# Attention and SwiGLU block: four pairs loaded in natural order and turned by TensorE, fewer transfers, reciprocals between transposes

## The chip, the core and the metric

The program runs on one core of one Trainium2 chip. A core has TensorE (PE), VectorE (DVE), ScalarE (ACT), GpSimd (POOL) and SyncE (SP), which only issues transfers here. Each engine works through its own instructions in the order in which they were written; semaphores order the engines among each other. The metric is device time in microseconds (us) of the core, the median of several runs.

## The reference

Normalised attention for 8 batches, 12 heads, 448 tokens and 64 features per head, and then a gated feed-forward layer over the 3584 tokens with 768 features (hidden width 1536). Cut to what is computed:

```
def rmsnorm(x, g):
    rms = np.sqrt(np.mean(x * x, axis=-1, keepdims=True) + 1e-06)
    return x / rms * g
q_n, k_n = (rmsnorm(q, g_q), rmsnorm(k, g_k))
scores = np.matmul(q_n, k_n.transpose(0, 1, 3, 2)) / np.sqrt(64)
scores = scores - np.max(scores, axis=-1, keepdims=True)
attn = np.exp(scores)
attn = attn / (np.sum(attn, axis=-1, keepdims=True) + 1e-09)
x = np.matmul(attn, v)            # then (B,H,S,D) -> (B*S, H*D)
g = x @ w_gate
out = (g / (1.0 + np.exp(-g)) * (x @ w_val)) @ w_out
```

Inputs and output are float32, but the three weight matrices arrive as float64.

## The kernel before

All work is in the function `fast`; `general` is another path, taken only if the gains are large, and does not run here.

**Pairs.** Two heads of one batch make a pair; `attention(m)` makes the work of pair m, of 48. The first 12 (`EARLY`) are done before any product of the feed-forward layer; the other 36 are spread among the down products of earlier blocks. Two batches form a block (`NB` is 4).

**One early pair.** `load` (L728) brings queries and keys in four transfers each, 56 KB apiece, in runs of 32 features (128 bytes), so that 32 tokens lie on 32 partitions and the head's feature halves in partition groups. `load_values` (L744, L747) brings values in four transfers. ACT squares both (L754), DVE sums over 32 features (L768), ACT swaps the sums of the feature halves between partition groups (L778), DVE adds them (L782). `inverse_root` takes a logarithm and an exponential on ACT (L678, L679) and improves the result on DVE (L684 to L686). POOL scales keys and queries (L795), DVE turns them in 32x32 blocks (L811), and ACT multiplies the queries by the gains (L814). Then come the scores on TensorE (L840) in four steps, the exponentials on ACT (L855), the weighted sums of the values (L916) and the sums of the weights (L947). DVE takes reciprocals of those (L982), TensorE spreads them over partitions (L990; in later pairs ACT does it, L1000), and the result is copied (L1005), joined (L1008) and divided (L1012) into `xs`.

**Buffers.** Queries and keys have four tiles (two pairs), values two, turned queries and keys two each. The score tile `st` has two buffers of two PSUM banks each; `at` for weighted sums has two of one bank; two more banks, `banks`, serve the sums of early pairs and later the gate products.

**Weights.** `convert` brings nine blocks of 128x128 float64 weights (1152 KB) in five transfers (L1136, L1138) into one of several places (`XS`, `GT`, `HS`, `ES`, `PAIRS`, `SPARE`), turns them into rounded float32 on ACT and DVE (L1146 to L1180), builds eleven sums and differences of blocks on POOL (L1199, L1202), and stores 15 "sides" to DRAM (L1227). There are 24 such pieces, sixteen for the up and eight for the down products; six of them are planned among the early pairs. A place can be used again when its sides are stored; some places wait for the last sums of the early pairs, since attention uses that memory.

**Blocks.** A 3x3 block product is done in 15 products. `block(n)` loads sides (L1288) in groups of five for the up products (L1328) and of two for the down products (L1502), and reads and combines the products on ACT and DVE.

**What sets the order.** The class `Order` keeps a list of pieces, each with an engine, an estimated time, a wished time (`when`) and a rank. A simulated run over these estimates picks, at each step, the piece that can start first, and ties go to the smaller `when - rank`. The instructions are written in the order in which it picks them, so an estimate changes the order, not only the prediction of it. `LEAD` is the planned start of the first pair, `PAIR` the planned time of an early one. Weight pieces of the early stage have rank 0, early pairs 60.

Of the kernel before, what the change touches and what calls it, by code (L numbers as in the profile page):

```python
# [477 lines left out]
def fast(  # L478
# [59 lines left out]
    EARLY = 2 * NPAIR  # L538

# [7 lines left out]
        qk=4, v=2, t=2, QT=2, KT=2, e=4, ea=7, eh=2, sums=1, inv=1, rd=1, rows=3, st=2, at=2, ss=2,  # L547
# [18 lines left out]
    def take(name, key, shape):  # L566
        if name in ("e", "ea"):
            at = order.turn[name] % BUFS[name]
            tiles[name, key] = es[:, at] if at < BUFS["e"] else more_es[:, at - BUFS["e"]]
            return tiles[name, key]  # L570
# [38 lines left out]
    UP_SUMS = (8, 1, 7, 13, 10, 14, 3, 5, 11, 0, 4)  # L609
    DOWN_SUMS = (1, 10, 14, 3, 11, 0, 4, 5, 8, 7, 13)  # L610
    BLOCKS = (6, 2, 12, 9)
# [16 lines left out]
    chosen = const.tile([P, 2, P], F32, name="chosen")  # L628
    gq2 = const.tile([P, 1], F32, name="gq2")
# [6 lines left out]
    LEAD, PAIR = 14.0, 9.0  # L636
# [35 lines left out]
    def inverse_root(m, sums, of, when, rank=0.0):  # L672


        def estimate():
            ss = of()
            rr = take("rr", m, list(ss.shape))
            nc.scalar.activation(rr, ss, AF.Ln, scale=GAIN**-2)  # L678
            nc.scalar.activation(rr, rr, AF.Exp, scale=-0.5)  # L679
# [18 lines left out]
    clusters = {}  # L698

# [3 lines left out]
    def attention(m):  # L703
# [19 lines left out]
        def load(x, src):  # L723
            def emit():
                to = take("qk", (m, x), [P, NC, C])
                for g in range(P // C):
                    rows = src[b, 2 * c + g // 2][:, ts(g % 2, C)]
                    queue.dma_start(to[ts(g, C)], rows.rearrange("(c i) f -> i c f", i=C))  # L728
# [5 lines left out]
                "ACT" if both else "SP", 1.4 if both else 2.4, ready - 28.0, emit, takes=[("qk", (m, x))], kb=224, early=25.0,  # L734
                after=[staged.get(PAIRS)],
            )

        loaded = [load(x, src) for x, src in enumerate((q, k))]
# [10 lines left out]
        load_v = add("SP", 2.4, ready - 16.0, load_values, takes=[("v", m)], kb=256, early=25.0)  # L749

        def square(x):
            if x == 0:
                take("t", m, [P, 2, NC, C])
            nc.scalar.activation(tiles["t", m][:, x], tiles["qk", (m, x)], AF.Square)  # L754
# [12 lines left out]
        def summed():  # L767
            nc.vector.tensor_reduce(  # L768
# [20 lines left out]
        sums = add("ACT", 0.9, ready - 16.0, swap, after=[sums], uses=[("ss", m)])  # L789
        sums = add("DVE", 0.15, ready - 15.0, both, after=[sums], uses=[("ss", m)])  # L790
        rr = inverse_root(m, sums, lambda: tiles["ss", m][:, 0], ready - 14.0, rank)

        def scale(x):
            rr = tiles["rr", m][:, ts(x, NC)].rearrange("p (c one) -> p c one", one=1)
# [13 lines left out]

        def transpose(x):
# [9 lines left out]
        kt = add(  # L819
# [3 lines left out]
        qt = add(  # L823
# [3 lines left out]
        qt = add(  # L827
# [81 lines left out]
        def weighted(j):  # L909
            for x in range(2):  # L910
# [4 lines left out]
                for h in range(2):  # L915
                    nc.tensor.matmul(  # L916
                        tiles["at", (m, x)][ds(D * h, D), queries],
                        tiles["v", m][rows, j, h],
# [39 lines left out]
        for j in range(NJ):  # L958
# [5 lines left out]
                uses=[weights_of(j), ("v", m)] + at * (j > 0),  # L964
# [16 lines left out]
        def invert():  # L981
            nc.vector.reciprocal(take("rd", m, [P, Q]), tiles[den])  # L982
# [27 lines left out]
        def divide():  # L1010
# [8 lines left out]
            "DVE", 1.52, when + 4.0, invert, after=[all_sums], uses=[] if of_bank else [den],  # L1019
            takes=[("rd", m)],  # L1020
# [99 lines left out]
    def convert(key, src, sums, to, when, place, by_bank):  # L1120

        rank = 20.0 if by_bank else 0.0
# [4 lines left out]
        raw, dst = places[place][:, 0 : 2 * VALUES], places[place][:, 2 * VALUES : PLACE]  # L1127
        words = raw.bitcast(U32).rearrange("p (n two) -> p n two", two=2)
        lo, hi = words[:, :, 0], words[:, :, 1]
        wait = [last_exp[0]] if place in (ES, PAIRS, GT[2]) else []  # L1130

        def load():

            to = raw.bitcast(I64).rearrange("p (b f) -> p b f", f=P)
            for i, n, rows in ((0, 2, (1, 3, 0)), (2, 2, (0, 2, 2)), (5, 3, (0, 3, 1))):
                nc.sync.dma_start(to[:, i : i + n], src(slice(*rows[:2]), rows[2]))  # L1136
            for i, k, n in ((4, 0, 0), (8, 2, 2)):
                nc.sync.dma_start(to[:, i], src(k, n))  # L1138

        loaded = add(  # L1140
            "SP", 2.5, when - 12.0, load, after=[staged.get(place), *wait], kb=1152, early=3.0
# [50 lines left out]
        b21, b31, b13, b23, b11, b12, b22, b32, b33 = (blocks[:, i] for i in range(9))  # L1192

        sides = places[place].rearrange("p (b f) -> p b f", f=P)[:, 7:22]
        at = {x: i for i, x in enumerate(sums)}
# [8 lines left out]
        def pair(x, i, j):  # L1204
            return x[:, i : j + 1 : j - i]
# [4 lines left out]
        for us, op in (  # L1210
            (0.79, plus(pair(sides, at[10], at[4]), pair(blocks, 5, 7), pair(blocks, 2, 8))),
            (0.79, plus(pair(sides, at[1], at[14]), twice(w[10]), pair(blocks, 0, 4))),
# [8 lines left out]
            (0.79, minus(pair(sides, at[11], at[0]), pair(blocks, 7, 8), pair(blocks, 2, 3))),  # L1221
# [56 lines left out]
    def load_sides(key, sides, part, sums):  # L1278
# [4 lines left out]
        for names, first in ((sums, 0), (BLOCKS, len(sums))):  # L1283
            here = sorted(names.index(x) for x in part if x in names)
            if here:
                size = len(here)
                src = sides[:, ds(first + here[0], size)]
                nc.sync.dma_start(to[:, ds(i, size)], src.rearrange("p x a b f -> p x (a b f)"))  # L1288
                i += size

    def place_of(x, part, sums):
        mine = [*(y for y in sums if y in part), *(y for y in BLOCKS if y in part)]
        return mine.index(x)
# [303 lines left out]
    for t, x in ((gq2, g_q), (gk2, g_k)):  # L1597
        col = x.rearrange("(d one) -> d one", one=1)
        nc.gpsimd.dma_start(t[0:64, :], col)
        nc.gpsimd.dma_start(t[64:128, :], col)  # L1600
    nc.vector.memset(chosen, 0.0)
# [96 lines left out]
```

## Time and profile before

| what | us |
|---|---|
| median of 3 runs | 1487.12 |
| lowest and highest | 1483.69, 1489.3 |
| span of the profiled execution, first to last instruction | 1484.0 |
| TensorE busy in it | 1425.0 (96%) |
| DVE, ACT, POOL busy | 916.0, 681.5, 414.1 |

The profile is of one further execution; its own device time is not listed apart from its span, which lies within the three runs. Busy time of TensorE counts from a matmul's start to its modelled end. A wait names the instruction that came last before the waiter could go on.

The order of the stages can be read off the timeline: no TensorE work until 14.66 us, the twelve early pairs until about 140 us, the up products of block 0 until about 330 us with most of the weight conversion beside them, then four stages in which down products and later pairs alternate with up products, and the last down products until about 1476 us.

### The profile page before, as it was taken

To read this page: it belongs to the slowest core of one execution; us is meant where nothing else is said; L and a number is where in the kernel's file an instruction comes from. 1 tells how busy PE (TensorE), PEld (TensorE's weight loads), DVE (VectorE), ACT (ScalarE), POOL (GpSimd) and SP (SyncE) were. 2 spreads that over 40 slices of the span, in tenths; PEclk is the share of its full clock that TensorE was granted. 3 is DMA by queue.
4 is the path that set the end of the run, shared out by engine and by line. 5 is a ranking of instruction groups with operands and counts; after the bars stand their busy time and mean duration, and the time that the engine had idled before them with its cause. 6 is when DMAs were issued, how large, how long until landed. Compare 5 with 4: busy or idle time off the path is not lost.

```text
span 1484.0 us, 19470 instructions
## 1 busy us (share of the span) xinstructions
PE 1425.0 (96%) x6672; PEld 675.4 (46%) x6672; DVE 916.0 (62%) x1405; ACT 681.5 (46%) x1366; POOL 414.1 (28%) x468
## 2 busy tenths in 40 slices
PE   5789999999999999999999999999999999999998
PEld 2334544443444455544444445554444445555553
DVE  4777887877978544355886733454786854432533
ACT  6774544437775322445767422354676532122100
POOL 2454586636444100012544200011343410000000
PEclk9999999999999999999999999999999999999999
DMA  7767999974453432533344432352353442222235
GB/s 165 158 144 236 292 308 341 296 219 90 99 115 85 113 106 71 138 103 90 74 111 110 100 117 73 106 136 77 96 119 85 90 119 89 80 98 73 83 98 107
DMA packets 415921, 193.30 MB, mean 130 GB/s; under 512 B 324164, under 2 KB 397892, under 8 KB 409668
## 3 DMA queue, kind: packets, MB, share of 16 engines
q1 hardware_dynamic: 402688, 190.35, 48.0%
q10 hardware_dynamic: 12996, 1.61, 0.7%
q8 instruction: 55, 0.90, 0.3%
q14 instruction: 54, 0.44, 0.1%
q0 software_dynamic: 128, 0.00, 0.0%
HBM read 157.29 MB, written 34.60 MB: 129 GB/s over the span
## 4 chain that ended last, share of the span: by engine, by line
PE 73%; DVE 3%; ACT 2%; issue 1%; DMA 1%; SPq 1%; ACTq 0%; DVEq 0%
PE mm L1502 22%; PE mm L1328 20%; PE at L1328 20%; PE st L840 6%; PE at L916 5%; PE st L947 1%; ACT spare L1000 1%; ACT es L855 1%; DVE rd L982 1%; DMA out_dram<-spare 0%; SPq L728 0%; DVE ss L782 0%; DMA work<-in_k_dram 0%; DVE ss L768 0%; DVE sums L866 0%
## 5 line engine op out<-in xcount | busy, mean ns | idle before, releaser
L1328 PE MATMUL mm<-xs,ws 128*128 128x448 f32 x960 | 401.2, 540 | 4.4 <-DVE spare L1276 2.2
L1328 PE MATMUL at<-xs,ws 128*128 128x448 f32 x960 | 400.6, 540 | 4.1 <-DVE v L1274 2.6
L1328 PEld LDWEIGHTS mm<-xs,ws 128*128 128x128 f32 x960 | 181.5, 190 | 185.8 <-issue 173.8
L1328 PEld LDWEIGHTS at<-xs,ws 128*128 128x128 f32 x960 | 181.9, 190 | 184.6 <-issue 172.6
L795 POOL TENSOR_TENSOR work<-work,rr 128x448 f32<-128x448 f32 x96 | 105.9, 1122 | 503.5 <-DVE rr L686 245.2
L840 PE MATMUL st<-work 64*64 64x448 f32 (+1 forms) x1536 | 155.1, 508 | 27.3 <-ACT work L814 21.2
L1502 PE MATMUL mm<-gt,ws 128*128 128x448 f32 x448 | 177.2, 545 | 0.0
L1272 DVE TENSOR_TENSOR gt<-gt,mm 128x448 f32<-128x448 f32 x64 | 39.7, 621 | 185.1 <-PE mm L1328 171.3
L1502 PE MATMUL mm<-hs,ws 128*128 128x448 f32 x384 | 152.1, 545 | 0.9 <-DVE ss L684 0.9
L855 ACT ACTIVATE es<-st 128x896 f32<-128x896 f32 x129 | 114.3, 913 | 56.1 <-PE at L916 42.8
L860 POOL TENSOR_TENSOR sums<-es 128x896 f32<-128x896 f32 x36 | 75.7, 2104 | 195.8 <-PE st L947 83.2
L1402 ACT ACTIVATE st<-gt 128x448 f32<-128x448 f32 x96 | 52.4, 547 | 163.8 <-DVE gt L1276 85.9
L1000 ACT COPY spare<-rd 32x224 f32<-32x224 f32 x288 | 108.1, 375 | 35.0 <-DVE rd L982 30.7
L1502 PEld LDWEIGHTS mm<-gt,ws 128*128 128x128 f32 x448 | 82.9, 190 | 84.2 <-issue 81.0
L916 PE MATMUL at<-es,v 64*64 64x448 f32 x1032 | 110.2, 545 | 7.2 <-ACT xs L1005 3.3
L1270 ACT COPY gt<-mm 128x448 f32<-128x448 f32 x80 | 42.5, 531 | 141.5 <-PE mm L1328 141.4
L1502 PEld LDWEIGHTS mm<-hs,ws 128*128 128x128 f32 x384 | 71.1, 190 | 72.9 <-issue 70.9
L840 PEld LDWEIGHTS st<-work 64*64 64x64 f32 x1536 | 50.9, 134 | 108.7 <-issue 38.1
L1270 ACT COPY v<-at 128x448 f32<-128x448 f32 x96 | 51.1, 532 | 83.2 <-PE at L1328 80.0
L860 POOL TENSOR_TENSOR sums<-sums,es 128x896 f32<-128x896 f32 x36 | 78.7, 2187 | 2.8
L811 DVE STREAM_TRANSPOSE work<-work 128x448 f32<-128x448 f32 x96 | 59.2, 627 | 25.2 <-POOL work L795 23.1
L916 PEld LDWEIGHTS at<-es,v 64*64 64x64 f32 x1032 | 39.7, 134 | 67.4 <-issue 57.4
(150 smaller groups left out, 1568.7 us busy)
## 6 DMA issues: line engine op xcount, KB each, us to landing
ws<-up_sides SPq DMA_DIRECT2D x32, 1024.0 KB, 4.9
ws<-down_sides SPq DMA_DIRECT2D x16, 1024.0 KB, 5.0
ws<-down_sides SPq DMA_DIRECT2D x28, 512.0 KB, 4.0
ws<-up_sides SPq DMA_DIRECT2D x16, 768.0 KB, 4.6
work<-in_q_dram SPq DMA_DIRECT2D x192, 56.0 KB, 2.4
work<-in_k_dram SPq DMA_DIRECT2D x188, 56.0 KB, 2.5
out_dram<-spare SPq DMA_DIRECT2D x168, 56.0 KB, 1.9
v<-in_v_dram SPq DMA_DIRECT2D x96, 96.0 KB, 2.5
```

The lines of the kernel that those rows point to most:

```text
L795: nc.gpsimd.tensor_tensor(out=tiles["t", m][:, x], in0=tiles["qk", (m, x)], in1=rr.to_broadcast([P, NC, C]), op=ALU.mult,)
L811: nc.vector.transpose(to, tiles["t", m][:, x].rearrange("p c f -> p (c f)"))
L840: nc.tensor.matmul(st[ds(D * x, D), h, 0:n], tiles["KT", m][rows, ds(P * j + D * of_keys, D)], tiles["QT", m][rows, ds(Q * of_queries, n)] ...
L855: nc.scalar.activation(e, tiles["st", (m, j)][:, :, 0 : S * width(j) // P], AF.Exp)
L860: nc.gpsimd.tensor_tensor(out=to, in0=tiles["e", (m, 0)] if j == 1 else to, in1=e, op=ALU.add)
L916: nc.tensor.matmul(tiles["at", (m, x)][ds(D * h, D), queries], tiles["v", m][rows, j, h], tiles["e", (m, j)][rows, h], start=j == 0, stop= ...
L1000: nc.scalar.copy(inv[ds(D * h + C * to, C), ts(x, Q)], tiles["rd", m][ds(D * h + C * x, C)])
L1270: nc.scalar.copy(to, ps)
L1272: nc.vector.tensor_tensor(out=to, in0=old, in1=ps, op=ALU.add)
L1328: nc.tensor.matmul(ps(), w[:, at, which, c], xs[:, SLOT[x], c], start=fresh and c == 0, stop=c == NC2 - 1, skip_group_check=True,)
L1402: nc.scalar.activation(take(*act, [P, 2, TB])[:, 0, 0:S], to, AF.Silu)
L1502: nc.tensor.matmul(banks[s][:, 0:S], w[:, at, s, g], where[x][:, g], start=fresh and g == 0, stop=g == NG - 1, skip_group_check=True,)
```

## The change

Six things are changed at once.

1. **Natural order for pairs 0 to 3.** Four tokens lie on one partition (112 partitions, each with 4 x 64 features of each head), so queries and keys are one transfer each, in runs of 1 KB. A token's features are on one partition, so nothing is swapped. POOL scales and sorts by token index, TensorE turns four 112x128 pieces of each into a PSUM tile `st`, and DVE (keys) and ACT (queries, with the gains) drain them.
2. **A few products ahead.** In pair 0, four products of the raw keys into a bank that nobody reads are issued on TensorE after the second square.
3. **Values for three pairs at a time** in the early stage: five transfers for three pairs, into `spare`.
4. **Weights in three transfers** per piece instead of five; raw and rounded parts change places, and the sides get another order, which gives fewer transfers in one of three groups of up sides. The sixth early piece goes to `GT[0]` instead of `SPARE`, which now waits for the last sums. Early weight pieces get rank 30.
5. **Reciprocals** (all 48 pairs): DVE turns the sums, takes reciprocals of seven columns, and turns them back, spread out.
6. `LEAD` is 10 instead of 14, and some estimates differ.

The core of the diff:

```diff
+    NATURAL = (0, 1, 2, 3)
+    R = S // NJ
...
-    UP_SUMS = (8, 1, 7, 13, 10, 14, 3, 5, 11, 0, 4)
-    DOWN_SUMS = (1, 10, 14, 3, 11, 0, 4, 5, 8, 7, 13)
-    BLOCKS = (6, 2, 12, 9)
+    UP_SUMS = (10, 14, 3, 8, 1, 7, 13, 5, 11, 0, 4)
+    DOWN_SUMS = (3, 10, 14, 1, 11, 0, 4, 5, 8, 7, 13)
+    BLOCKS = (6, 9, 2, 12)
...
-    LEAD, PAIR = 14.0, 9.0
+    LEAD, PAIR = 10.0, 9.0
...
+                if natural:
+                    to = take("qk", (m, x), [R, 2, NJ * D])
+                    rows = src[b][2 * c : 2 * c + 2].rearrange("h (p j) d -> p h (j d)", j=NJ)
+                    queue.dma_start(to, rows)
+                    return
...
+        def load_six():
+            x = take("ve", m // 3, None)
+            for j in range(NJ):
+                for p in (0, D) if j == NJ - 1 else (0,):
+                    n = D if j == NJ - 1 else P
+                    rows = v[b][2 * c : 2 * c + 6, ds(P * j, n)].rearrange("h s d -> s h d")
+                    nc.sync.dma_start(x[ds(p, n), j], rows)
...
+            nc.scalar.activation(tiles["t", m][:, x], of, AF.Square)
+            if m == 0 and x:
+                for _ in range(4):
+                    nc.tensor.matmul(banks[0], chosen[0:R, 0], of, start=True, stop=True)
...
+        def turn(x):
+            if x:
+                take("st", (m, "turned"), [P, 2, TB])
+            turned = tiles["st", (m, "turned")][:, x]
+            for j in range(NJ):
+                nc.tensor.transpose(turned[:, ts(j, R)], tiles["t", m][:, x, ts(j, P)], ident[0:R, 0:R])
+
+        def drain(x):
+            turned = tiles["st", (m, "turned")][:, x, 0:S].rearrange("p (j r) -> p r j", j=NJ)
+            to = take("KT" if x else "QT", m, [P, S]).rearrange("p (r j) -> p r j", j=NJ)
+            if x:
+                nc.vector.tensor_copy(out=to, in_=turned)
+            else:
+                nc.scalar.activation(to, turned, AF.Copy, scale=gg)
...
         def invert():
-            nc.vector.reciprocal(take("rd", m, [P, Q]), tiles[den])
+            rd, rc = take("rd", m, [P, Q]), take("rc", m, [P, Q // C])
+            nc.vector.transpose(rd, tiles[den])
+            nc.vector.reciprocal(rc, rd.rearrange("p (c i) -> p c i", i=C)[:, :, 0])
+            every = rc.rearrange("p (c one) -> p c one", one=1).to_broadcast([P, Q // C, C])
+            nc.vector.transpose(rd, every)
...
-        rank = 20.0 if by_bank else 0.0
+        rank = 20.0 if by_bank else 30.0
...
-            for i, n, rows in ((0, 2, (1, 3, 0)), (2, 2, (0, 2, 2)), (5, 3, (0, 3, 1))):
-                nc.sync.dma_start(to[:, i : i + n], src(slice(*rows[:2]), rows[2]))
-            for i, k, n in ((4, 0, 0), (8, 2, 2)):
-                nc.sync.dma_start(to[:, i], src(k, n))
+            for at, n in ((slice(3, 8, 2), 0), (slice(0, 3), 1), (slice(8, 3, -2), 2)):
+                nc.sync.dma_start(to[:, at], src(slice(0, 3), n))
...
-    turns = [(*XS, *GT[:2], HS, SPARE), (ES, PAIRS, GT[2], SPARE, HS), (ES, PAIRS, HS, SPARE), (ES, HS)]
+    turns = [(*XS, *GT[:2], HS, GT[0]), (ES, PAIRS, GT[2], SPARE, HS), (ES, PAIRS, HS, SPARE), (ES, HS)]
```

## The prediction

> **What bounds the kernel now.** I read busy time by stretches first, because the change sits almost wholly in the first twelve pairs. Columns: stretch, length, then busy time and count for PE, weight loads, DVE, ACT and POOL, granted clock, DMA share, GB/s.
>
> ```profile
> 0.00:15.00 15.00, 0.34 (x4) 0.30 (x8) 5.62 (x18) 6.55 (x18) 4.72 (x14) 1.00 0.67 114
> 15.00:140.00 125.00, 105.21 (x1196) 46.51 (x1189) 94.56 (x156) 86.24 (x163) 61.80 (x93) 0.99 0.72 174
> 140.00:333.00 193.00, 185.75 (x492) 92.37 (x490) 156.90 (x236) 86.00 (x122) 112.42 (x218) 1.00 0.95 292
> 333.00:400.00 67.00, 63.70 (x434) 26.37 (x438) 57.06 (x79) 50.99 (x119) 39.28 (x24) 1.00 0.46 97
> 400.00:1400.00 1000.00, 993.44 (x4353) 471.49 (x4346) 569.42 (x880) 447.49 (x937) 195.86 (x120) 1.00 0.38 98
> ```
>
> From 400 to 1400 us TensorE rests 6.6 us in all, so nothing there can give much. It rests 14.7 us before its first product, 19.8 us in the twelve early pairs (15 to 140), 7.3 us in the first up products, and 7.4 us in the tail of stores. Those first two are where the change can act. Next, the lead, from the timeline (start, length, engine, line):
>
> ```profile
> 5.85 0.58 ACT L754 ACTIVATE work<-work 128x448 f32<-128x448 f32 x1 [2.96 <-DMA work<-in_k_dram]
> 7.15 0.58 ACT L754 ACTIVATE work<-work 128x448 f32<-128x448 f32 x1 [0.73 <-DMA work<-in_k_dram]
> ...
> 8.88 0.88 ACT L778 COPY ss<-ss 32x28 f32<-32x28 f32 x4 [1.15 <-DVE ss L768]
> ...
> 11.39 1.83 POOL L795 TENSOR_TENSOR work<-work,rr 128x448 f32<-128x448 f32 x2 [7.79 <-DMA v<-in_v_dram]
> ...
> 12.50 1.40 DVE L811 STREAM_TRANSPOSE work<-work 128x448 f32<-128x448 f32 x2
> ...
> 13.94 0.67 ACT L814 ACTIVATE work<-work,gg 128x448 f32<-128x448 f32 x1 [0.44 <-DVE work L811]
> ```
>
> One serial chain, begun by a load. Then what TensorE waited for from 14 to 140 us (total, times, longest; the 14.7 is the lead):
>
> ```profile
> PE st L840 <- ACT work L814: 21.2, 6, 14.7
> PE at L916 <- ACT xs L1005: 3.3, 2, 2.3
> PE at L916 <- DVE xs L1008: 2.7, 2, 2.1
> PE at L916 <- ACT gt L855: 2.3, 2, 1.3
> PE mm L990 <- DVE rd L982: 2.0, 2, 1.3
> ```
>
> ACT is named, but is it the cause? The timeline around the stall at 44.39 (2.10 us) shows ACT standing still for a load, and SP issuing that load late:
>
> ```profile
> 36.90 4.15 SPq L728 DMA_DIRECT2D work<-in_k_dram  x4
> ...
> 41.50 0.58 ACT L754 ACTIVATE work<-work 128x448 f32<-128x448 f32 x1 [1.01 <-DMA work<-in_q_dram]
> 43.20 0.58 ACT L754 ACTIVATE work<-work 128x448 f32<-128x448 f32 x1 [1.13 <-DMA work<-in_k_dram]
> 43.69 0.65 ACT L814 ACTIVATE work<-work,gg 128x448 f32<-128x448 f32 x1
> ```
>
> Pair 3's queries stood on ACT behind pair 4's squares. Summed over its timeline, SP spends 111.0 of the first 128 us issuing (55.5 of the first 60): 54.8 on 92 queries-and-keys transfers, 31.6 on 48 of values, 17.9 on 30 of weights. SP's queue is what the early pairs wait for underneath; DVE (94.6 of 125) is next.
>
> [...] pair 0's first 448-column records take 951 ns, later ones 536; about 4 us of half speed lose 2.0. [...]
>
> **The change, part by part.**
>
> *Lead.* A pair's tensor becomes one transfer of 1 KB runs, not four of 128 B. Queries: issued by 0.76 + 0.57 (4.58 / 8), plus the 2.8 us from last issue to square today (3.05 to 5.85): 4.1. Keys on ACT: 1.63 + 0.57 + 2.8 = 5.0. Second square 0.58 x 512/448 = 0.66, to 5.7. Reduction 1.09 x 1024/896 = 1.25, to 7.0. The swap (0.88) goes; a small add of 0.19 takes the place of L782. Root and its three corrections, 10.02 to 11.17 today, to 8.5. POOL 0.92 x 512/448 = 1.05 each: keys 9.7, queries 10.7. The warm-up (4 products of 512 columns; L1328 gives 0.376 a record of 448, two records each) costs 3.4 us warm and 6.9 cold, 5.5 when 4 us are cold: 5.0 to 10.5. It stands ahead of the first transposes in PE's order: keys turned 10.5 to 11.5, queries to 12.4, ACT's drain 0.66, scores at about **13.0** instead of 14.66: 1.7 won, plus the 2.0 of half clock, since the array is then warm. Identity building on POOL (after its fourth gain transfer, 3.6) has until 9.7; were that cover gone, each us is a us.
>
> *TensorE's transposes.* Four a turn. Nearest row: L990, 128x128 weights by 224 columns, four records in 0.95 us (28.22 to the next), 0.24 each. One record per transpose gives 0.95 a turn, two give 1.9. I take 0.95 [...], so 1.9 a pair; pairs 1 to 3 add **5.7**, at worst 11.4. Pair 0's lie in the lead.
>
> *SP.* Queries and keys lose 21 issues x 0.60 = 12.5; values go from 48 issues to 4 x 5, 28 x 0.66 = 18.4; six weight pieces lose two each, 12 x 0.60 = 7.2. Some 38 of 111 us leave the queue. What is late next is DVE.
>
> *DVE and ACT.* Each reciprocal (1.55) becomes two 224-wide transposes (0.627 / 2 + some 0.02, so 0.33) and a 7-column reciprocal (0.19, like the small L684): 0.87, 0.68 less; twelve times, 8.2. Natural pairs swap two DVE turns (1.25) for one copy (0.64): 2.4. ACT loses four swaps, 3.5. DVE falls from 94.6 to some 84. Bounds of the triple: 0.6 to 1.6, so from 11 won to nothing.
>
> *TensorE's rests, 15 to 140.* L814: 6.5 without the lead (21.2 - 14.7). Of these 5.5 are stalls at 21.28, 33.29, 44.39 and 58.33 (0.85 + 0.29 + 2.10 + 2.58, less some 0.3 kept), all behind late loads: gone. L855 loses half (1.2), L982 loses 0.6 twice (1.2). L1005 and L1008 (6.0, ACT and DVE late between pairs 4 and 7) lose half, 3.0. Together 10.9, leaving 8.9. If only the load stalls go, 14.3 stay; if nearly all go, 3.
>
> *End of the early stage.* 13.0 + 105.2 - 2.0 + 5.7 + 8.9 = **130.8** against 140.0: 9.2 won.
>
> *Later.* Weight conversions after the early pairs wait for the last sums (SP waited 9.0 us for L947), so block 0's preparation shifts with it. Three transfers carry the same bytes as five: nothing, hidden by a DMA share of 0.95; SP's spared issuing there has no taker. The regrouped sides save one transfer in each up triple: nothing, since TensorE waited 0.9 us for these. The placing of the sixth weight piece in GT[0] makes it wait for the first piece's store; if it is late, 1 to 3 us. Steady state: L982 delayed L840 by 1.3 us in all: 1.3 won. Total 10.5.
>
> Span 1484.0 - 10.5 = 1473.5. The median shown is 1487.1, 3.1 above the span, so **1476.6**.
>
> **The rivals.**
> - *Absorbed in block 0.* The pairs end early, but the weights (0.95 of the DMA engines from 140 to 333) set the pace, and TensorE waits for sides instead. For: share and 292 GB/s. Against: only 0.9 us of such waits now, and a rigid shift. Some 3 us left: 1484.
> - *Fuller.* Rests fall to about 2 and no transposes' cost is visible: 7 more than mine, and up to 3 of DVE relief: 1467. For: SP and DVE both relieved. Against: ACT still in order between squares and exponentials.
> - *Slower: the turned pair holds a score tile.* Both turns write one of the two two-bank tiles `st`, from the first transpose to ACT's drain, over 3 us with the queries' scaling between. Scores and exponentials then alternate on one tile: 0.76 + 0.92 + 0.3 instead of 0.95 a step, 1.05 x 4 steps = 4.2 a pair, and with two records per transpose 1.9 more: 6.1 x 4 = 24 against 10.5 won: about 1500. It decides from 10.5 / 4 = 2.6 us a pair. For: PE is in order, and only two tiles. Against: weighted sums and totals can run meanwhile, and TensorE has 20 us of rest.
>
> **How the numbers follow.** Mine 0.50 (its own range 1470 to 1482: transposes twice as dear +5.7, rests -6 to +5), absorbed 0.18, fuller 0.16, slower 0.16. 0.5% is 7.4 us, about what a measurement can tell from no change; faster means below 1479.7. Mine is that nine times in ten (0.45), fuller always, so 0.61, with a little of the absorbed 0.62; same 0.22; slower 0.16. Range 1464 to 1488: it leaves out the slower case and little of the fuller.
>
> **What would show it.** First scores near 13 us and records of 536 ns there; transposes near 0.24 us each; SP issuing some 73 us in the early stage; three DVE instructions of 0.87 for each reciprocal; first up product near 131 us; unchanged rests from 140 to 333, shifted. Wrong if scores wait for `st`, if the first up product is past 138, or if TensorE waits for sides in block 0.

## The result

The changed kernel takes 1496.66 us (median of 4 runs, 1495.01 to 1499.16) against 1486.19 us of the kernel before on the same chip (4 runs, 1483.69 to 1489.3). The ratio is 1.0065, with a 95% interval of 1.0053 to 1.0077: slower by some 9.7 us, where 10.5 us less were predicted. The profiled execution of after has a span of 1494.0 us, before one of 1484.0.

First the same stretches as for before (stretch, length, busy time and count of PE, weight loads, DVE, ACT, POOL, granted clock, DMA share, GB/s):

```profile
0.00:15.00 15.00, 6.05 (x16) 2.94 (x16) 5.71 (x16) 4.45 (x9) 5.44 (x16) 1.00 0.85 176
15.00:140.00 125.00, 105.58 (x1124) 46.66 (x1124) 86.10 (x174) 81.49 (x150) 63.88 (x94) 0.95 0.73 183
140.00:333.00 193.00, 180.79 (x545) 89.44 (x544) 144.28 (x219) 84.90 (x114) 111.46 (x216) 0.96 0.87 269
333.00:400.00 67.00, 64.36 (x375) 27.46 (x377) 55.71 (x87) 48.58 (x109) 31.19 (x20) 1.00 0.46 104
400.00:1400.00 1000.00, 996.29 (x4431) 475.28 (x4424) 557.38 (x964) 460.55 (x963) 202.31 (x125) 1.00 0.39 100
```

DVE's relief is there (94.6 to 86.1 us in the early pairs), but TensorE still rests 19.4 us from 15 to 140, does 1124 records there instead of 1196, and has less of its clock (0.95 against 0.99). From 140 to 333 both clock and DMA share are lower than before (0.96 and 0.87 against 1.00 and 0.95).

The lead, from the timeline of ACT and TensorE (start, length, engine, line, what ended the rest):

```profile
8.48 1.15 ACT L795 ACTIVATE work<-work 112x512 f32<-112x512 f32 x2 [3.70 <-DMA work<-in_k_dram]
16.06 0.63 ACT L889 ACTIVATE work<-st,gg 128x448 f32<-128x448 f32 x1 [1.65 <-DVE gg L1709]
...
8.59 5.28 PE L798 MATMUL mm<-work,chosen 112*128 112x512 f32 x8 [8.59 <-DMA work<-in_k_dram]
13.71 0.93 PE L881 MATMUL st<-ident,work 112*128 112x112 f32 x8
16.75 1.36 PE L940 MATMUL st<-work 64*64 64x224 f32 x16 [2.11 <-ACT work L889]
```

The keys' square came at 8.48, not at 5.0; both turns took 0.93 us together; and the queries were drained 1.4 us after the turns, since DVE made the product of the gains, `gg`, only at 15.80. Then what TensorE waited for from 14 to 140 us (total, times, longest):

```profile
PE at L1016 <- DVE xs L1112: 7.3, 3, 3.4
PE st L940 <- ACT work L889: 3.3, 3, 2.1
PE st L940 <- ACT es L955: 2.4, 1, 2.4
PE mm L1094 <- DVE rd L1086: 1.7, 1, 1.7
...
PE st L940 <- ACT work L896: 1.0, 2, 0.6
```

The waits behind late loads (6.5 us in before, without the lead) are mostly gone: L889 and L896 now give 2.2 us without the lead. The 2.4 us for L955, at 24.31, are partly of the same kind, since ACT made this exponential only after pair 2's squares, which had waited 1.0 us for their loads. New is DVE's join, L1112, 7.3 us. And the tail of the early pairs, from the timelines of five engines:

```profile
119.49 1.84 POOL L862 TENSOR_TENSOR work<-work,rr 128x448 f32<-128x448 f32 x2
164.84 2.09 POOL L1304 TENSOR_TENSOR hs<-hs 128x256 f32<-128x256 f32 x3 [29.12 <-DVE hs L1282]
...
140.30 0.62 DVE L1116 TENSOR_TENSOR xs<-xs,mm 128x448 f32<-128x448 f32 x1 [1.12 <-PE mm L1094]
140.84 1.17 DVE L893 STREAM_TRANSPOSE work<-work 128x448 f32<-128x448 f32 x2
...
142.76 5.51 PE L940 MATMUL st<-work 64*64 64x224 f32 x32 [2.49 <-ACT work L896]
207.99 3.32 PE L1429 MATMUL mm<-xs,ws 128*128 128x448 f32 x4 [8.96 <-DVE st L1270]
...
136.38 19.24 SPq L1240 DMA_DIRECT2D es<-in_moe_w_val_dram  x3
...
199.77 1.17 SPq L1389 DMA_DIRECT2D ws<-up_sides  x2
```

Pair 11 was scaled by POOL at 119.49 to 121.3, but DVE turned it only at 140.84, behind pair 10's division (140.30), because it was written there. So its last sums ended at 154.4, where before they ended at 139.3. SP stood 19 us at the first late weight piece, whose place those sums set free, and POOL had nothing to add up for 29 us (18 in before). Block 0 then began at 148.20 instead of 140.13, and rested 8.96 us at 208. The trace names a DVE instruction there, but the loads of the products' sides were only issued by SP at 199.77.

Where the whole time went, from the starts of the first scores and of the first up product of each block in TensorE's timeline (us; the last column is the span):

| kernel | first scores | to first up product | block 0 | block 1 | block 2 | remainder | span |
|---|---|---|---|---|---|---|---|
| before | 14.66 | 125.5 | 364.9 | 350.2 | 350.4 | 278.3 | 1484.0 |
| after | 16.75 | 131.5 | 371.8 | 347.8 | 347.8 | 278.4 | 1494.0 |
| predicted difference | -1.7 | -7.5 | 0 | -1.3 in both | | 0 | -10.5 |
| difference | +2.1 | +6.0 | +6.9 | -2.4 | -2.6 | +0.1 | +10.0 |

The border between the second and third stage is not the same in both kernels: in after TensorE does 5.4 us of early pairs' work behind the first up product (pair 11's weighted sums and their spreading), in before 0.9. So 4.5 of the 6.9 us are pair 11's own work, and the early pairs are later by more than the table says.

Longer rests alone do not explain the loss. In the whole span TensorE rests 54.5 us in after and 59.0 in before, but it is busy for 1439.5 us instead of 1425.0. Some 8.5 of these 14.5 us are new work: 6.05 us before the first scores, where before has 0.34, and three turned pairs at 0.93. The remainder is mostly clock. After the first scores the trace of before grants half the clock for one stretch of 3.4 us; in after there are five stretches, and TensorE works for 22.5 us in them. A score record of 448 columns takes 951 ns in them, 536 outside. Half of the difference, 9.5 us, is an estimate of what this costs; pair 0's start at half speed in before, 2.0 us, has to be taken off. The last two stretches lie at the rests of the seam (after; columns as above, the clock is the third number from the end):

```profile
140.00:150.00 10.00, 7.51 (x42) 2.47 (x40) 4.53 (x8) 3.96 (x5) 0.00 (x0) 0.66 0.19 55
200.00:210.00 10.00, 2.01 (x3) 1.17 (x4) 9.32 (x14) 2.93 (x3) 7.10 (x15) 0.65 1.04 362
210.00:220.00 10.00, 10.00 (x23) 4.77 (x22) 9.33 (x13) 4.89 (x8) 9.37 (x20) 0.84 1.09 356
```

The other three begin beside rests of 2.44, 3.45 and 3.18 us, which end at 24.31, 114.6 and 129.5.

### The profile page after: what moved, and what is told of

It reads as the page before. It is cut to its first block, busy times and chain, and to the rows that moved or that the text cites. A ratio compares the mean times of both kernels' runs of the same rounds, so it can differ in the third digit from the quotient of the medians.

```text
span 1494.0 us, 19412 instructions
## 1 busy us (share of the span) xinstructions
PE 1439.5 (96%) x6712; PEld 685.1 (46%) x6712; DVE 885.2 (59%) x1497; ACT 685.8 (46%) x1354; POOL 414.3 (28%) x470
## 4 chain that ended last, share of the span: by engine, by line
PE 73%; DVE 2%; ACT 1%; DMA 1%; issue 1%; SPq 0%; ACTq 0%; DVEq 0%
PE mm L1603 22%; PE mm L1429 19%; PE at L1429 19%; PE st L940 6%; PE at L1016 6%; PE st L1047 1%; DMA out_dram<-spare 1%; ACT spare L1104 1%; SPq L743 0%; DVE spare L1651 0%; ACT es L955 0%; DMA work<-in_k_dram 0%; DVE ss L821 0%; ACT work L896 0%; DVE gt L1506 0%
## 5 line engine op out<-in xcount | busy, mean ns | idle before, releaser
L862 POOL TENSOR_TENSOR work<-work,rr 128x448 f32<-128x448 f32 x88 | 95.8, 1108 | 489.2 <-DVE rr L695 350.0
L955 ACT ACTIVATE es<-st 128x896 f32<-128x896 f32 x129 | 114.2, 915 | 57.3 <-PE at L1016 47.7
L1016 PE MATMUL at<-es,v 64*64 64x448 f32 x864 | 88.2, 537 | 0.0
L893 DVE STREAM_TRANSPOSE work<-work 128x448 f32<-128x448 f32 x88 | 54.2, 628 | 22.0 <-POOL work L862 19.0
L795 ACT ACTIVATE work<-work 128x448 f32<-128x448 f32 (+1 forms) x96 | 54.4, 578 | 26.6 <-DMA work<-in_q_dram 14.2
```

The costliest lines, as they stand in the source:

```text
L795: nc.scalar.activation(tiles["t", m][:, x], of, AF.Square)
L862: nc.gpsimd.tensor_tensor(out=tiles["t", m][:, x], in0=tiles["qk", (m, x)], in1=rr.to_broadcast([P, NC, C]), op=ALU.mult,)
L893: nc.vector.transpose(to, tiles["t", m][:, x].rearrange("p c f -> p (c f)"))
L955: nc.scalar.activation(e, tiles["st", (m, j)][:, :, 0 : S * width(j) // P], AF.Exp)
L1016: nc.tensor.matmul(tiles["at", (m, x)][ds(D * h, D), queries], values(rows, j, h), tiles["e", (m, j)][rows, h], start=j == 0, stop=j == NJ ...
```

## The experiments

Each kernel ran beside the kernel before; the ratio is to that one, with its 95% interval. A trace shows one execution, and several of those used below lie well off their kernel's median: 1491.35 us for pair 11 with the store (median 1487.78), 1490.38 for the repaired seam (1486.64), 1501.47 for the first kernel with piece 10 held (1497.84), 1481.78 for the reciprocals alone (1484.67).

**1. The seam between the early pairs and block 0.** First pair 11 alone:

```diff
-                "POOL", 1.0, ready - 9.0, lambda x=x: scale(x), after=[rr], port=True,
+                "POOL", 1.0, ready - 9.0 - 40.0 * (m == 11), lambda x=x: scale(x), after=[rr], port=True,
```

> The changed kernel with one wish time altered: the scaling of pair 11's queries and keys on POOL is wished 40 us earlier, so that the pair is written out ahead of pair 10's last steps. Theory A (order): in the changed kernel pair 11 is turned only at 140.84 us, SP stands before the first late weight piece until 155.68, and TensorE later waits 9.0 us for sides; with the pair earlier SP's block ends near 140, the 9.0 us wait shrinks to under 3, and the time falls from 1496.7 by 8 to 14 us, to about 1486. Theory B (the new work itself, transposes on TensorE and their score tile, is what costs): the early pairs 0 to 3 are untouched by this edit, so the time stays within 3 us of 1496.7.

Measured: 1492.12 us, ratio 1.0047 (1.0029 to 1.0064). By the medians that is 4.5 us less than after, not 8 to 14, and the interval overlaps that of after. The last sums ended at 138.6 and the first up product began at 139.39, as early as in before; and then block 0 stood still. Timelines of ACT, TensorE and SP in that run:

```profile
161.35 0.97 ACT L1372 COPY gt<-mm 128x448 f32<-128x448 f32 x2 [0.30 <-DMA up_sides<-gt]
...
161.94 3.36 PE L1429 MATMUL mm<-xs,ws 128*128 128x448 f32 x4 [14.66 <-ACT gt L1372]
...
148.53 3.21 SPq L1240 DMA_DIRECT2D hs<-in_moe_w_val_dram  x3
151.85 0.97 SPq L1329 DMA_DIRECT2D up_sides<-gt  x1
```

The sixth early piece lies in `GT[0]`, where block 0 puts its first gate products. ACT may copy them only when the piece's sides are stored, and SP issued this store (151.85) behind five weight loads. The next kernel adds a wait in the plan, so that the store is written ahead of loads of `ES`, `PAIRS`, `GT[2]` and `SPARE`:

```diff
-        wait = [last_exp[0]] if place in (ES, PAIRS, GT[2], SPARE) else []
+        wait = [last_exp[0], staged.get(GT[0])] if place in (ES, PAIRS, GT[2], SPARE) else []
```

> The kernel after with two edits: the queries and keys of the last early pair (11) are scaled 40 us earlier in the plan, and the loads of the weight pieces that wait for the last early sums also wait, in the plan, for the store of the sixth early piece, so that SP issues this store before them. Computes everything. In the run with the first edit alone (1492.1 us) the last sums were done at 138.6 us, but ACT could copy the first gate product of block 0 only at 161.35, when the sides of the sixth piece had left GT[0] (its store was issued at 151.85, behind five weight loads); TensorE rested 14.66 us. Theory A (the written order at the seam of the two stages): first up product at 139 to 141, the rest of 14.66 gone or below 3 us, the block ends 10 us earlier, time 1481 (1477 to 1485). Rival (the weights are prepared too slowly, whatever the order): the rest moves to a later group of up products, and the time stays at 1489 to 1493.

Measured: 1487.78 us, ratio 1.0005 (0.9996 to 1.0014): 4.3 us less than with pair 11 alone, not 11. The rest for `GT[0]` fell to 3.33, but a new one came, as the rival said. TensorE and SP in that run:

```profile
203.76 3.32 PE L1429 MATMUL mm<-xs,ws 128*128 128x448 f32 x4 [9.18 <-DMA ws<-up_sides]
...
162.93 0.56 SPq L1329 DMA_DIRECT2D up_sides<-hs  x1
177.34 0.56 SPq L1329 DMA_DIRECT2D up_sides<-es  x1
184.57 0.55 SPq L1329 DMA_DIRECT2D up_sides<-work  x1
```

Piece 10 (in `hs`) had been prepared ahead of pieces 6 and 7 (`es`, `work`), which the second group of up products needs; in before these two are stored at 165.12 and 171.50. My next step was to make piece 10 wait as well (`if by_bank` instead of the list of places), with the other two edits and by itself:

> As the run with pair 11's scaling and the sixth piece's store moved, and one more edit: every weight piece after the sixth waits in the plan for the last early sums, the one in HS (number 10) too, so that it no longer goes ahead of pieces 6 to 9. Computes everything. In the run without this edit (1487.8 us) the rest of 14.66 us had become 3.33 at 152.5 and 9.18 at 203.8; the stores of sides came in the order 10, 6, 7, 8 at 162.9, 177.3, 184.6, 192.5, where before has 6, 7, 8 at 165.1, 171.5, 181.1. Theory A (piece 10 takes DVE and POOL while 6 and 7, which the second group of up products needs, stand behind it): stores of 6 and 7 at 165 to 172, the rest at 203.8 below 4 us, time 1480 (1477 to 1485). Rival (DVE and transfers are the limit, the order only moves the rest): rests of 9 us or more in all between 150 and 345, time 1487 or more.

> The kernel after with that last edit alone: piece 10 in HS waits in the plan for the last early sums like 6 to 9. Computes everything. Pair 11 and the sixth piece's store are as in after in the plan. Theory A: last sums as late as in after (154) or some us earlier, but the rest of 8.96 us at 208 is below 4 us, time 1490 (1486 to 1493). Rival (the late pair alone costs the time, by holding SP until 154): 1495 to 1498, the rest stays above 7 us.

Measured: 1497.84 (1.0067, 1.0054 to 1.008) and 1507.54 (1.0149, 1.0132 to 1.0165). The theory fell in both, and the rivals were right that the rests stay: the stores came in the right order, and TensorE still rested 9.99 and 9.11 us. ACT and POOL in the first of the two show why:

```profile
159.94 1.25 ACT L1248 ACTIVATE es<-es 128x1152 f32<-128x1152 f32 x1
...
168.82 2.08 POOL L1304 TENSOR_TENSOR es<-es 128x256 f32<-128x256 f32 x3 [29.03 <-ACT gt L1248]
```

Piece 6's conversion on ACT was now written behind eight copies of block 0 and began at 159.94; in before it stands behind four and begins at 147.72. Putting the loads in order had moved ACT's order. So the last kernel of this group was chosen by its written order as a whole: pair 11 early, the sixth piece's store ahead of the loads, piece 10 behind piece 9, and piece 6 converted behind three copies. Three edits gave that, with all of the change kept:

```diff
-        rank = 20.0 if by_bank else 30.0
+        rank = 20.0 if by_bank else 45.0 if key == ("up", 5) else 30.0
...
-                "POOL", 1.0, ready - 9.0, lambda x=x: scale(x), after=[rr], port=True,
+                "POOL", 1.0, ready - 9.0 - 40.0 * (m == 11), lambda x=x: scale(x), after=[rr], port=True,
...
-        "DVE", 0.2, 9.0,
+        "DVE", 0.2, 3.0,
```

> The kernel after with pair 11 scaled 40 us earlier in the plan, the sixth early piece at rank 45 instead of 30, and gg planned at 3 us. All of the change is kept. In the written order the sixth piece's store now comes before the loads of pieces 6 to 9, piece 10 comes after them, and piece 6's conversion on ACT stands behind three copies of block 0. Computes everything. Theory A: no rest for GT[0], sides of piece 6 stored at 163 to 168 as in before, no rest over 3 us in block 0, time 1480 (1476 to 1485). Rival (whatever the order, the stage of block 0 takes 8 us more with this change): 1488 to 1493.

Measured: 1486.64 us, ratio 1.0 (0.9991 to 1.0008), 10.0 us below after and level with before. There is no rest for `GT[0]`, and none over 2.3 us while the up products run. SP's stores of pieces 6 and 7 in that run:

```profile
163.64 0.56 SPq L1329 DMA_DIRECT2D up_sides<-es  x1
171.45 0.55 SPq L1329 DMA_DIRECT2D up_sides<-work  x1
```

The operations are those of after, so it is shown that the order cost the ten microseconds. That the rest of the change gains is not shown, since 1480 was expected. Nor is it shown how the ten divide among the stages, since the traced execution is the slowest of this kernel's 13.

**2. The start and the values.** The values of six heads planned later (`early=25.0` to `early=2.0` for these transfers), `gg` earlier with the four products on raw keys left out, and values pair by pair with the sixth piece back in `SPARE`, without and with pair 11's edit:

> The changed kernel with the groups of values allowed only 2 us ahead of their wished time instead of 25, so that the second group does not follow the first at once. Theory A (order and a crowded start): pair 0's keys land before 6 us instead of 8.5, first scores at about 14 instead of 16.75; the order of the later pairs changes too, and pair 11 comes earlier; together 1484, within 5. Theory B (transposes cost): first scores come earlier by 2 to 3 us and the whole by no more than that, 1494.

> As the run with pair 11's scaling and the sixth piece's store moved, and further: the product of the two gains (gg) is planned at 3 us instead of 9, and the four products on raw keys ahead of the first scores are left out (their result is read by nobody). Computes everything that the output needs. If the lead is lost to gg and to these products as the trace of after suggests (queries drained at 16.06 us, waiting for gg that came at 15.80; turns at 13.71 behind products that end at 13.87), the first scores start at 15.2 to 15.6 instead of 16.75 and the time falls by 1 to 2 us against the run without these edits. Rival: without the products ahead TensorE's clock is low longer at the start of pair 0, which eats the gain: the same time, or up to 2 us slower.

> The kernel after with the values of early pairs loaded pair by pair as before, in four transfers each, and with the sixth early weight piece in SPARE again, which then waits for no sums. Nothing else; pair 11's turn is still planned behind pair 10's join. Computes everything. Theory A (the time is lost because pair 11's turn on DVE stands behind pair 10's, and SP and ACT behind its sums): little changes, 1491 to 1496, last sums after 148 us. Rival (grouped values and the place of the sixth piece cost the time): last sums near 140, 1481 to 1486.

> As the run with values by pair, and pair 11's queries and keys scaled 40 us earlier in the plan. The sixth piece is in SPARE, its store is still planned behind four weight loads. Computes everything. Theory A with the place GT[0] as the cause of the rest of 14.66 us in the run with pair 11 alone: no such rest here although the store is late, last sums at 136 to 139, time 1480 (1476 to 1484). Rival (late store means too few prepared weights, whatever the place): a rest of over 8 us in the first 30 us of block 0, time 1489 to 1493.

Measured: 1492.58 (1.0041, 1.0028 to 1.0054); 1491.06 (1.003, 1.002 to 1.004); 1498.23 (1.0079, 1.0065 to 1.0093); 1494.88 (1.0057, 1.0045 to 1.007). With five of the ten value transfers moved away from the start, the first scores came at 17.38, no earlier than 16.75: what was gained by that edit came from the tail (last sums at 146.0, not 154.4). The second run started its scores at 16.97, 1.0 earlier than its partner (17.98), and took 3.3 us more. The third is as slow as after, with last sums again at 154.4, so grouped values are not the cause of the late tail. Its first scores came at 15.04, 1.7 earlier than in after, and its first up product at 148.24, no earlier than there. The fourth had no rest for `GT[0]`, as expected, but last sums at 144.3, and took 3.3 us less than the third, where 1480 was expected: half a miss. In these runs a microsecond at the start is not passed on, and each edit moves the order elsewhere.

**3. The parts in one order.** Two parts on the kernel before, the order of instructions held by leaving the plan's estimates as they were:

> The kernel before with the reciprocals between transposes alone; the planner's estimate stays 1.52, so every engine keeps its order. Theory A: 1.55 us becomes about 1.0 on DVE for each pair, DVE has slack almost everywhere: 1486.2 less 1 to 4, about 1484. Theory C (the triple is slower in place, since three dependent instructions follow each other on DVE): slower by 2 or more, 1488 or above.

> The kernel before with the weights in three transfers, the other layout of a place and the other order of sides alone; estimates, ranks and places stay, so every engine keeps its order. Theory A: same bytes in the same place, some 25 us of issuing less on SP, 1486.2 within 3 us. Theory D (the weights' new form is what costs the 9 us of waiting for sides): 1491 or above.

Measured: 1484.67 (0.9986, 0.9979 to 0.9994) and 1488.82 (1.0017, 1.0009 to 1.0025). Then the whole change with what steers the plan as before (`LEAD` 14, rank 0, values by pair, sixth piece in `SPARE`):

> The kernel after with what steers the plan as before: LEAD 14, early weight pieces at rank 0, values by pair, the sixth piece in SPARE that waits for no sums. What stays of the change: pairs 0 to 3 in natural order with turns on TensorE, weights in three transfers, reciprocals between transposes. In this plan pair 11 is turned before pair 9's join and piece 10 is loaded behind 6 to 8. Computes everything. Theory A (the new operations save time and only the written order costs it): last sums at 130 to 136, no rest over 4 us in block 0, time 1479 (1475 to 1484). Rival (turned pairs hold the score tile or cost TensorE more than they save): last sums at 139 or later, time 1487 or more.

Measured: 1491.91 (1.0033, 1.0021 to 1.0045): better than after by 4.8, but not below before. So natural pairs alone, then with reciprocals, then with the weights in three transfers, all three with one order of instructions:

> The kernel before with pairs 0 to 3 in natural order and the four products on raw keys, nothing else of the change (values by pair, five transfers, old reciprocals, LEAD 14, rank 0, the sixth piece in SPARE). Computes everything. Theory A (written order): natural pairs save TensorE's rests among the first pairs (15.5 us in before, 7.6 in after) and cost 0.95 us a turned pair; last sums at 133 to 137, time 1482 (1478 to 1486). Rival B (natural pairs cost as much as they save: a start 2 to 3 us later, turns, the clock): last sums at 139 or later, 1486 to 1492.

> As the run with natural pairs alone, and the reciprocals between transposes, with the plan's estimate left at that of the old ones, so that the order of instructions is the same. Computes everything. All theories: 1 to 3 us less than natural pairs alone, as reciprocals alone gave 2 us on the kernel before.

> As the run before it in this group, and the weights in three transfers with the new order of sides, again with the same order of instructions. Computes everything. If the three transfers cost what they cost alone (2.5 us on the kernel before), 1 to 4 us more than natural pairs and reciprocals; rival (their cost came from one collision in the old order): within 1 us.

Measured: 1490.1 (1.0017, 1.001 to 1.0024), 1487.53 (1.0007, 0.9999 to 1.0016) and 1490.73 (1.0026, 1.0014 to 1.0038). By the ratios the reciprocals gain 1.5 us here and 2.1 alone; the three transfers cost 2.8 here and 2.5 alone; natural pairs cost 2.5. In the two steps from run to run here the intervals overlap; each part measured alone against before has an interval clear of 1. The stages of these runs, as in the table above:

| kernel | first scores | to first up product | block 0 | block 1 | block 2 | remainder |
|---|---|---|---|---|---|---|
| reciprocals alone | 14.58 | 123.6 | 363.8 | 349.8 | 349.9 | 278.3 |
| weights alone | 14.58 | 126.2 | 365.4 | 350.4 | 350.2 | 280.1 |
| natural pairs alone | 17.10 | 122.0 | 372.2 | 350.2 | 348.7 | 278.3 |
| all three parts | 16.40 | 119.9 | 373.9 | 349.8 | 349.8 | 279.3 |
| seam repaired | 17.10 | 124.9 | 372.7 | 347.8 | 347.8 | 278.3 |

Natural pairs do part of what they should: from first scores to first up product they save 3.5 us, and with the other two parts 5.6. But their first scores come 2.4 and 1.7 us later than in before, so the first up product is only 1.0 and 3.8 us earlier. And block 0, which has none of their operations, takes 7 to 9 us longer in the three kernels of this table that have them, and 363.8 and 365.4 us, as in before, in the two with the order of before. In the run with all three parts pieces 6 and 7 are stored 3.8 us earlier than in before, just as far as the first up product is; the gain is there until about 284 us (sides stored at 283.73 against 286.65), and goes at the end of block 0. TensorE in that run:

```profile
286.22 1.77 PE L1429 MATMUL mm<-xs,ws 128*128 128x448 f32 x4 [1.69 <-DVE gt L1376]
316.67 3.21 PE L1429 MATMUL mm<-xs,ws 128*128 128x448 f32 x4 [2.76 <-DVE gt L1374]
336.10 2.03 PE L940 MATMUL st<-work 64*64 64x224 f32 x16 [2.70 <-ACT work L896]
```

Four records of 448 columns take 1.77 us after a rest of 1.69 and 3.21 after one of 2.76: the second rest is followed by half the clock, which the trace grants for 3.41 us. This does not always follow. The same rest in the run with natural pairs alone left the speed as it was:

```profile
318.60 1.77 PE L1429 MATMUL mm<-xs,ws 128*128 128x448 f32 x4 [2.76 <-DVE gt L1373]
```

Rests and clock together account for the longer block 0. From its first up product to that of block 1 TensorE rests 11.7 us in before, and 15.9, 16.5 and 15.4 in the three kernels of this table with natural pairs; it works at half clock for none in before, and for 6.8, 9.7 and 8.8 us in these. The longer rest plus half of that time gives 7.6, 9.6 and 8.1 us, where the table has 7.3, 9.0 and 7.8.

The rest at 336 waits for pair 12's queries, whose scores stand there ahead of the first down product of block 0; before has three down products ahead of them:

```profile
329.71 2.42 PE L1502 MATMUL mm<-hs,ws 128*128 128x448 f32 x6
333.05 7.00 PE L1502 MATMUL mm<-hs,ws 128*128 128x448 f32 x18 [0.92 <-DVE ss L684]
339.98 1.36 PE L840 MATMUL st<-work 64*64 64x224 f32 x16
```

**4. Can the change win?** The repaired kernel with weights in five transfers again (same order), and that with one more down product written ahead of pair 12's scores:

```diff
-                after=[kt, qt, staged.get(ES), before],
+                after=[kt, qt, staged.get(ES), before, *(down_products.get((0, 6), [])[1:] if m == EARLY else [])],
```

> As the run with the seam repaired (1486.6 us), with the weights in five transfers and the order of sides as before; the order of instructions is the same. Computes everything. If the three transfers cost 2.5 to 3 us here too: 1484 (1482 to 1486). Rival: within 1 us of 1486.6.

> As that run, and pair 12's first scores are planned behind the second down product of block 0, so that TensorE has two down products to do, not one, before it waits for pair 12's queries (its rest of 3.36 us at 343 in the run with the seam repaired; before has three there and rests 0.97). Computes everything. If these rests at the end of block 0, with the lower clock after them, are what is given back there: 1 to 4 us less than the run without this edit. Rival: the rest comes back a little later, within 1 us.

Measured: 1487.53 (1.0008, 1.0 to 1.0016) and 1485.88 (0.9997, 0.9989 to 1.0005). In this order the three transfers cost nothing (1486.64 with them), as the rival said, so their 2.5 to 2.8 us belong to the order they were in, and what exactly they collide with there is open. The further down product gave 1.65 us between the medians, with intervals that overlap; in the trace it did what it was for:

```profile
334.47 4.00 PE L1606 MATMUL mm<-hs,ws 128*128 128x448 f32 x10 [0.51 <-DVE hs L1153]
338.83 1.36 PE L940 MATMUL st<-work 64*64 64x224 f32 x16 [0.36 <-ACT work L896]
341.70 1.80 PE L940 MATMUL st<-work 64*64 64x448 f32 x16 [1.51 <-ACT more L955]
```

The rest of 3.36 in its partner became 0.36 and 1.51, the mean clock from 340 to 360 us rose from 0.91 to 1.00, and block 0's segment fell from 371.9 to 369.2. In the whole segment the rests did not fall (15.6 and 16.2 us); what went is 6.8 us of work at half clock. The fastest kernel of all, and the only one whose interval lies wholly below 1, is the kernel before with the reciprocals alone, 1484.67.

## Why the prediction was wrong

**The step that failed** is "block 0's preparation shifts with it", together with "End of the early stage ... 130.8": both take the order of the work as given. The summand for TensorE's rests was read off an order that the change itself rewrites, since each new estimate, rank and place goes through the plan. In after this put pair 11's turn behind pair 10's division: last sums at 154.4, not near 131. The front of block 0 then did not shift rigidly, because SP, ACT, DVE and POOL have their own written orders there: SP issued the loads of the sides late, and TensorE rested 8.96 us for them. With only the order mended the time fell by the ten microseconds that after had lost (1486.64).

A second term stood at nothing: half clock after pair 0. Between first scores and first up product after works for 17.1 us at half clock, before for 3.4. In the sum to 130.8 the misses are therefore chiefly some 11 us of rests, an estimated 7 of clock (half of 17.1, less half of the 3.4 in before) and 3.75 of lead; the transposes were 2.9 us cheaper than put down. Two of the signs that the prediction named for being wrong came true: the first up product past 138, and TensorE waiting for sides in block 0. And the mended order only brought the loss back, not the forecast gain: in every kernel with natural pairs block 0 is longer by 4 us or more than in before, by its rests and, in all but the last kernel, by half clock.

Point by point:

- *Lead, 13.0:* 16.75. The keys' square came 3.5 us late (8.48, not 5.0), and `gg` in DVE's queue, which has no summand, cost 1.4; together that is more than the 3.75 us missed, because the other summands were a little too dear. The early products went from 1061 to 592 ns a record, and the eight turning records behind them took 0.93 us, against 2.01 in the run without these products. Pair 0's first 16 score records took 1.36, as the forecast had it (448 columns in 536 ns), and 2.52 in that run; but 2.40 and 2.52 also in two runs with the products, the repaired seam and the plan of before. So the gain is not sure to last to the scores, and a faster start did not reach the end in any run.
- *Transposes, 1.9 a pair:* 0.93 a pair, so one record each, of about 0.12 us. Even the lower of my two values was twice too high.
- *SP:* 111.0 us of issuing in the first 128 fell to 83.4, not to 73.
- *Reciprocals:* three instructions of 0.41, 0.20 and 0.41, 1.02 us instead of 0.87. Alone they gain 2.1 us, where their two items, 1.2 and 1.3, make 2.5. Right in kind and in size.
- *Rests, 8.9 from 15 to 140:* 19.4. The load stalls mostly went, as reasoned; DVE's join and the late pair took their place. With the plan of before and the same natural pairs, reciprocals and weights, first scores came at 16.40 and the first up product 119.9 us later, near the 117.8 that 130.8 - 13.0 makes. That is in part luck: TensorE rested 14.3 us there, not 8.9, and cheaper transposes made up for about half of that.
- *Place of the sixth piece, 1 to 3 us "if late":* the collision was another than the one named, with block 0's first gate products, and cost 14.66 us of rest once pair 11 was early.
- *Blocks 1 and 2:* each 2.4 to 2.6 shorter, more than the 1.3 in all predicted; the reciprocals with their order held give 0.4 to 0.5 a block, so most of this is the new order as well.
- *From span to median, 3.1:* the profiled execution of after took 1495.76 us with a span of 1494.0, so 1.8 is the difference within one execution. This item is 1.3 us too large.
- *Rivals:* the score tile held by a turned pair was not it (TensorE rested 0.7 us in all ahead of turns in the early pairs, and 3.8 ahead of scores for an exponential, L955, where 4.2 a pair were put down; and natural pairs shorten their stage). That 1496.66 lies near its 1500 is luck. "Absorbed in block 0" had the place right, since TensorE did wait for sides at 208, but not the reason: over the whole stage the DMA share fell from 0.95 to 0.87, so transfers were not its limit; they were issued late, and then crowded, with a share of 1.04 from 200 to 210.

Not settled: why three transfers cost in one order and not in another, and which pieces of the plan bring the longer rests of block 0 in the runs with natural pairs.

## What to carry to other kernels

If a planner's estimates write the order of the queues, a change of an operation's cost is two changes, and the second can be larger: kernels with the same operations took from 1486.64 to 1507.54 us here. Compare the order itself at every seam between stages, for each engine, before summing savings. To price an operation, hold the order and swap only the operation. When one engine is busy 96% of the time, as here, a gain of some microseconds in one stage can be lost at the next seam if a single queue has its first instruction there no earlier. And count the busy engine's clock beside its rests: a rest that brings half the clock costs more than its length (2.76 us in the run with all three parts, then 3.41 us at half clock: an estimated 1.7 more).

## What the runs showed that was not expected

- A short rest of TensorE can cost more than its length, but does not always. In the 19 traces of this case, from 20 us on, half clock lies beside or within 4 us behind all 28 rests of 3 us and more, and 32 of the 53 between 2 and 3 us; in those of before and after alone, behind all three (3.18, 3.45 and 8.96 us) and three of the six (2.06, 2.44 and 2.49, but not 2.10, 2.29 and 2.58). A rest of 2.76 us was followed by four records in 3.21 us in one run and in 1.77 in another; one of 2.49 in after by 32 score records in 5.51 us, which took 3.38 in before after a rest of 0.70 (in after another rest, of 1.72, lay 3 us earlier). The half-clock stretches in which TensorE works last 3.41 us in before, and 3.41, 6.83 or 10.24 in after.
- A DVE transpose of 128x224 takes 0.41 us, more than half of one of 128x448 (0.63): not quite proportional.
- Pair 0's keys, a transfer of 224 KB issued by ACT at 1.62, took 6.8 us to land in after, and 6.2 with half of the value transfers moved away; in before four of 56 KB took 3.2 each. Grouped values seem to be part of it: the keys' square came at 6.65 to 7.72 in the six kernels with natural pairs and values pair by pair, at 7.33 to 8.53 in the ten with groups. The rest was not isolated.
